# A retention layer with a feed-forward layer behind it: the order of three group sums on VectorE, and the place of one weight difference on GpSimd

## The chip, the cores and the metric

The kernel runs on one core of a Trainium2 chip. A core has a matrix engine (TensorE, PE in the profile), a vector engine (VectorE, DVE), a scalar engine (ScalarE, ACT), a general engine (GpSimd, POOL) and an engine that issues transfers (SyncE, SP). Each runs its own instructions in order; they wait for one another on semaphores. SBUF is the memory on the core that all of them read, PSUM the one into which TensorE accumulates. The metric is the time of one execution on the device, in microseconds (us), as the median of several runs.

## The reference

The inputs are q, k and v of 4 batches, 8 heads, 768 positions and 64 channels, and the weights of a feed-forward layer, 512 to 2048 to 512. What is computed:

```python
gamma = 1.0 - 2.0 ** (-5.0 - np.arange(H))
for t in range(S):
    state = gamma * state + outer(k[:, :, t], v[:, :, t])
    y[:, :, t] = scale * einsum('bhd,bhde->bhe', q[:, :, t], state)
x = y.transpose(0, 2, 1, 3).reshape(B * S, H * D)      # 3072 tokens x 512
h = x @ w_in
g = np.maximum(h, 0.0) + alpha * np.minimum(h, 0.0)
out = g @ w_out
```

The inputs and the output are float32; inside, the kernel multiplies in float16.

## The kernel before, in words

The 3072 tokens are cut into 24 units of 128 tokens and 6 blocks (n = 0 to 5) of 512 tokens. For each unit the retention part is done in chunks: scores within the chunk, masked, and a running state between chunks. Its result is written as xT, the input of the feed-forward layer for that block. The feed-forward layer of a block has two stages: `h = x @ w_in` with the activation, which leaves `gt` (2048 channels by 512 tokens, kept as 16 tiles f of 128 channels), and `g @ w_out`. The retention work of block n + 1 is woven into the second stage of block n.

The second stage of blocks 1 to 5 (`seven`, L802) is a product of 2 x 2 quarter matrices made with seven products in place of eight. `gt` is cut into four quarters: tokens 0 to 255 or 256 to 511 (`t0`, `t1`), and channel tiles 0 to 7 or 8 to 15 (`f`, `f8`). The seven products need four sums of these quarters, made by `g_sums(n, part, which, eng)` (L782): sum 0 is (`t1`, `f`) plus (`t1`, `f8`); sum 1 is sum 0 less (`t0`, `f`); sum 2, called `third`, is (`t0`, `f`) less (`t1`, `f`); sum 3 subtracts sum 1 from (`t0`, `f8`) in place. In the profile the tiles of sums 0 and 1 are called `gs`. `part` is 0 or 1 for half of the channel tiles, or None for all. `eng` is the engine, V for VectorE and G for GpSimd. `seven` asks first for two products that need no sum (32 matmuls), then for the product of sum 1 (16 matmuls: four of part 0, four of part 1, and the same again for the next 128 tokens), then for that of sum 0.

The first stage of blocks 3 to 5 (`ffn1_mix`, L918) treats a quarter of the channel tiles in the same way, and for that needs four differences and sums of w_in, which are made once (`win_sum(i, eng)`, L889, tile `wins`), and four differences of x for each block (`x_sum`, L902, tile `xsum`). The steps run in the order of the list `MIX`; its steps 5 and 6 read `wins` 0 and 1, step 7 reads `wins` 2, and step 3, the eleventh of the list, reads `wins` 3. GpSimd finishes three pairs of activations for these steps (two instructions each, L1002 and L1008).

All sums, of `gt`, of w_in and of x, go through one helper with one instruction, so all of them stand at L757 in the profile:

```python
def minus(eng, out, a, b, op=SUB):
    eng.tensor_tensor(out=out, in0=a, in1=b, op=op)
```

The order of the work on each engine is the order in which the program text issues it; no planner changes it. What a waiting instruction holds up is what is written behind it for the same engine. The places that matter here:

- In block 1, GpSimd makes sum 0 of part 0 (L1268) while the last activations of the block are still on VectorE. VectorE then makes sum 1 of part 0, sum 0 of part 1 and sum 1 of part 1 (L1313 to L1316). Blocks 2 to 4 make sums 0 and 1 whole on VectorE, with `part` None.
- In block 2, GpSimd makes the third sum of part 0 (L1291) and then the four differences of w_in (L1292).
- At the end of block 2's second stage, VectorE makes differences 0 and 1 of block 3's x, and GpSimd differences 2 and 3 (L1410 to L1413). What GpSimd does next is in block 3: the scaling of k and q of its last unit, behind which SP issues that unit's transpose and the loads of the next four units; then the three pairs of activations; then the third sum of part 0.

Of the kernel before, what the change touches and what calls it, by code (L numbers as in the profile page):

```python
# [19 lines left out]
def kernel(  # L20
# [72 lines left out]
    def bank(i, name, dt=FP, n=512):  # L93
        return psp.tile([128, n], dt, tag=f"p{i % 4}", bufs=1, name=name)
# [59 lines left out]
    def turn(u):  # L154
        kqT[u] = sbp.tile([128, 8, 128], F16, tag="kt", bufs=4, name=f"kt{u}")
        nc.sync.dma_start_transpose(
            out=kqT[u], in_=kqs[u].rearrange("p a i r d -> p (a i r d)")
        )
# [469 lines left out]
    def ffn1(n, lo=0, fts=None):  # L628
        for ft in fts or range(lo, NFT):
            hps = ps("hps", tag="pb")  # L630
            for hp in range(4):
                nc.tensor.matmul(  # L632
                    out=hps,
                    lhsT=w_in_all[:, hp, 128 * ft : 128 * ft + 128],
                    rhs=xT[n][:, :, hp, :],
                    start=(hp == 0),
                    stop=(hp == 3),
                )
                if hp == 3:
                    hm = sbp.tile([128, TB], FP, tag="hm", bufs=3, name="hm")  # L640
                    nc.scalar.activation(out=hm, in_=hps, func=RELU, bias=0.0, scale=-1.0)  # L641
                    nc.vector.scalar_tensor_tensor(  # L642
                        out=gt_at(n, ft, slice(0, TB)),
                        in0=hm,
                        scalar=oma_sb[:, ft : ft + 1],
                        in1=hps,
                        op0=MULT,
                        op1=ADD,
                    )
                yield  # L650
# [105 lines left out]
    def minus(eng, out, a, b, op=SUB):  # L756
        eng.tensor_tensor(out=out, in0=a, in1=b, op=op)  # L757
# [131 lines left out]
    def win_sum(i, eng):  # L889
        if not wins:  # L890
            wins.append(sbp.tile([128, 4, 2, 256], F16, tag="gs2", bufs=1, name="wins"))
        t = wins[0]
        a = [[w_in_all[:, 2 * l : 2 * l + 2, 1024 * j : 1024 * j + 256] for l in range(2)] for j in range(2)]
        x, y, op = (
            (a[1][0], a[1][1], ADD),
            (t[:, 0], a[0][0], SUB),
            (a[0][0], a[1][0], SUB),
            (a[0][1], t[:, 1], SUB),
        )[i]
        minus(eng, t[:, i], x, y, op=op)  # L900

    def x_sum(n, i, eng=nc.vector):  # L902
        if not xsum:
            xsum.append(sbp.tile([128, 4, 2, 256], F16, tag="gs3", bufs=1, name="xsum"))
        t = xsum[0]
        b = [[xT[n][:, j, 2 * l : 2 * l + 2, :] for j in range(2)] for l in range(2)]
        x, y = (
            (b[0][1], b[0][0]),
            (b[1][1], t[:, 0]),
            (b[1][1], b[0][1]),  # L910
            (b[1][0], t[:, 1]),
        )[i]
        minus(eng, t[:, i], x, y)
# [109 lines left out]
    def flush(late):  # L1023
        while late:
            late.pop(0)()

    def tick(gen, m):
        for _ in range(m):
            if next(gen, 1) == 1:
                return  # L1030
# [60 lines left out]
    V, G, A = nc.vector, nc.gpsimd, nc.scalar  # L1091
# [182 lines left out]
    for n in range(1, NBLK):  # L1274
        more = n + 1 < NBLK
        u0 = UB * (n + 1)
        if n == 2:
            gen = ffn1(n, fts=[HF * (f % 2) + f // 2 for f in range(NFT)])
            tick(gen, 8)
            flush(late_stores)  # L1280
            tick(gen, 6)
            for i in range(UB):
                scaled(u0 + i, "k", G)
                scaled(u0 + i, "q", G)
                turn(u0 + i)
                cast(u0 + i, G)

                for u in ((), (0,), (), (1, 2, 3))[i]:
                    load(u0 + u + UB)
                tick(gen, (14, 14, 6, 16)[i])  # L1290
            g_sums(n, 0, 2, G)  # L1291
            for i in range(4):  # L1292
                win_sum(i, G)
            for _ in gen:
                pass
        elif n > 2:
            gen = ffn1_mix(n)
            tick(gen, 8)
            flush(late_stores)
            if more:  # L1300

                scaled(u0 + 3, "k", G)
                scaled(u0 + 3, "q", G)
                turn(u0 + 3)
            for u in range(u0 + UB, min(u0 + 2 * UB, NU)):
                load(u)
            for _ in gen:
                pass
        if more:
            us = [u0, u0 + 1]  # L1310
            pq = scores(us)
            states(us)
        for p, w in (  # L1313
            ((0, 1), (1, 0), (1, 1)) if n == 1 else ((None, 0), (None, 1)) if more else ((1, 0), (1, 1))
        ):
            g_sums(n, p, w, V)  # L1316
        gen = seven(n)
        if not more:
            tick(gen, 4 * HF + 2)
            g_sums(n, 0, 2, V)  # L1320
            g_sums(n, 1, 2, V)
            g_sums(n, 0, 3, V)
            g_sums(n, 1, 3, V)
        if more:
            pa, pb = [u0, u0 + 1], [u0 + 2, u0 + 3]
            if n > 2:
                for u in pb:
                    cast(u, A)


            nxt = [u for u in range(u0 + UB, u0 + UB + 3) if n > 1 and u < NU]

            def chain(us, pq, first=(), between=(), last=(), ticks=0):
                sums(us[0])
                for g in first:
                    g_sums(n, *g)
                tick(gen, ticks)
                masked(us, pq)
                for g in between:
                    g_sums(n, *g)  # L1340
                for u in last:
                    scaled(u, "q", G)
                    turn(u)
                sums(us[1], late=n > 1 and us is pb)

            if n > 1:

                chain(pa, pq, [(1, 2, G)], ticks=4 * HF + 2)
                for u in nxt[0:1]:
                    scaled(u, "k", A)  # L1350
                tick(gen, 26)
                g_sums(n, 0, 3, G)
            else:
                tick(gen, 4 * HF // 2 + 1)
                scaled(11, "q", A)
                turn(11)
                for u in range(12, 16):
                    load(u)
                cast(10, A)
                cast(11, A)  # L1360
                tick(gen, 16)
                g_sums(n, 1, 3, G)
                chain(pa, pq, between=[(0, 2, V)])
                g_sums(n, 1, 2, V)
                tick(gen, 31)


            y = [bank(turns[0] + 2, "ya"), bank(turns[0] + 3, "yb")]
            out_first(pa, y)
            for X in range(2):  # L1370
                nc.scalar.activation(
                    out=seen[:, 8 * X : 8 * X + 8],
                    in_=y[X][:, 63:512:64],
                    func=COPY,
                    bias=0.0,
                    scale=1.0,
                )
            if n > 1:
                pq = scores(pb)
                states(pb)  # L1380
                out_second(pa)
            else:
                states(pb)
                out_second(pa)
                pq = scores(pb)
            if n > 1:
                chain(pb, pq, [], [(1, 3, G)], nxt[0:1])
            else:
                chain(pb, pq)
                g_sums(n, 0, 3, G)  # L1390
            tick(gen, 6)
            for u in nxt[0:2]:
                cast(u, A)
            for u in nxt[1:3]:
                scaled(u, "q", G)
            if n > 1:
                tick(gen, 15)
                decay(pb[1])
            for u in nxt[1:2]:
                scaled(u, "k", A)  # L1400
                turn(u)
            tick(gen, 17 if n > 1 else 23)
            out_first(pb, z=[ps("za"), ps("zb")])
            out_second(pb)
            for u in nxt[2:3]:
                scaled(u, "k", A)
                turn(u)
            tick(gen, 7)
            if n > 1:
                x_sum(n + 1, 0)  # L1410
                x_sum(n + 1, 1)
                x_sum(n + 1, 2, G)
                x_sum(n + 1, 3, G)  # L1413
        for _ in gen:
            pass
    flush(late_stores)
# [30 lines left out]
```

## Time and profile before

| what | us |
|---|---|
| median of 3 runs | 197.99 |
| the three runs | 197.58, 197.99, 487.58 |
| the profiled execution, its own time | 198.98 |
| span of the profiled execution, from its first to its last instruction | 197.0 |
| TensorE busy in that span | 189.3 |
| VectorE busy | 151.3 |
| GpSimd busy | 147.5 |
| ScalarE busy | 121.7 |

TensorE's granted clock is 1.000 over the whole span. The profiled execution's own time is 1.98 us longer than its span, which is what lies around the first and the last instruction. Rows of the timeline give the start in us from the span's begin, the length in us, the engine, the line, the operation, the tile written and the tiles read, the shape and the count; the bracket gives the idle time before the row and what ended it. Several instructions of one kind in a row are merged into one row, whose length runs from the start of the first to the end of the last.

### The profile page before, as it was taken

What the parts mean: (1) busy time and instruction counts of PE and PEld (TensorE: products, weight loads), DVE (VectorE), ACT (ScalarE), POOL (GpSimd) and SP (SyncE); (2) the same over time, 40 slices, a digit from 0 to 9 for tenths busy, and PEclk for the clock granted to TensorE, in tenths of its full rate; (3) what the DMA queues carried; (4) which work ended last, traced back from release to release, by engine and by line L of the source; (5) the groups of instructions that cost most, each with busy time, mean ns of one, the idle gap of its engine ahead of it and who ended that gap; (6) DMA issues with size and microseconds to landing.
All of it is one profiled execution on the core that took longest, in us unless ns stands there. A gap on an engine that the chain in (4) does not pass through costs nothing.

```text
span 197.0 us, 6461 instructions
## 1 busy us (share of the span) xinstructions
PE 189.3 (96%) x2668; PEld 131.7 (67%) x2668; DVE 151.3 (77%) x260; ACT 121.7 (62%) x272; POOL 147.5 (75%) x148
## 2 busy tenths in 40 slices
PE   7789899999999989999999999999999999999993
PEld 5657444557768878744688754788754888654882
DVE  2597889253999698588897879968879977799943
ACT  3368664349687863476458988749987433687120
POOL 3286788999996955999659999579999397589000
PEclk9999999999999999999999999999999999999999
DMA  6999999999999989899999999993890011200014
GB/s 168 310 336 350 404 396 296 332 358 179 210 230 148 214 257 272 196 215 299 196 231 228 226 185 265 237 221 93 113 263 2 3 57 63 100 3 0 2 57 160
DMA packets 92749, 38.78 MB, mean 197 GB/s; under 512 B 70176, under 2 KB 88624, under 8 KB 92720
## 3 DMA queue, kind: packets, MB, share of 16 engines
q1 hardware_dynamic: 91440, 37.36, 77.2%
q10 hardware_dynamic: 1280, 1.01, 1.5%
q8 instruction: 21, 0.34, 0.7%
q14 instruction: 8, 0.07, 0.1%
HBM read 27.35 MB, written 6.29 MB: 171 GB/s over the span
## 4 chain that ended last, share of the span: by engine, by line
PE 73%; SPq 10%; DMA 7%; POOL 6%; DVE 1%; issue 1%; POOLq 0%
PE ops L809 30%; PE hps L942 16%; PE hps L632 12%; PE hps L972 5%; SPq L340 4%; SPq L117 4%; DMA wi<-in_moe_w_in_dram 4%; PE ops L734 4%; POOL wsum L757 3%; DMA kqs<-in_q_dram 3%; PE ya L293 1%; PE yb L293 1%; POOL gs L757 1%; DVE gs L757 1%; POOL ukq L354 1%; PE sca L234 1%
## 5 line engine op out<-in xcount | busy, mean ns | idle before, releaser
L809 PEld LDWEIGHTS <-gt 128*128 128x128 f16 x320 | 30.6, 98 | 4.2
L942 PE MATMUL hps<-xT,win 128*128 128x512 f16 x144 | 33.0, 379 | 0.0
L929 DVE SCALAR_TENSOR_TENSOR gt<-hm,small,hps 128x512 f16<-128x512 f32 (+1 forms) x42 | 28.7, 706 | 5.1 <-ACT hm L925 3.8
L809 PE MATMUL ops<-wout,gt 128*128 128x256 f16 x240 | 28.4, 273 | 0.0
L925 ACT ACTIVATE hm<-hps 128x512 f32<-128x512 f32 x39 | 23.1, 593 | 6.1 <-PE hps L942 5.4
L632 PE MATMUL hps<-xT,win 128*128 128x512 f16 x112 | 24.7, 379 | 0.6 <-POOL win L1073 0.6
L137 POOL TENSOR_TENSOR kq<-kqs,tab 128x512 f16<-128x512 f32 x23 | 23.7, 1051 | 1.9 <-DMA kqs<-in_q_dram 1.9
L642 DVE SCALAR_TENSOR_TENSOR gt<-hm,small,hps 128x512 f16<-128x512 f32 x28 | 20.9, 748 | 3.8 <-ACT hm L641 0.9
L942 PEld LDWEIGHTS <-win 128*128 128x128 f16 x144 | 14.1, 98 | 14.5
L641 ACT ACTIVATE hm<-hps 128x512 f32<-128x512 f32 x28 | 16.7, 597 | 8.9 <-PE hps L632 8.6
L674 DVE SCALAR_TENSOR_TENSOR gt<-hm,small,hps 128x256 f16<-128x256 f32 x40 | 16.9, 476 | 5.0 <-ACT hm L669 5.0
L827 ACT ACTIVATE kept<-ops 128x512 f32<-128x512 f32 x15 | 9.0, 597 | 18.8 <-PE ops L809 18.7
L632 PEld LDWEIGHTS <-win 128*128 128x128 f16 x112 | 10.9, 98 | 13.6 <-POOL win L1073 1.1
L809 PE MATMUL ops<-wsum,gs 128*128 128x256 f16 x160 | 19.0, 273 | 0.7 <-DVE gs L757 0.7
L217 POOL TENSOR_TENSOR t<-ss,tab 128x256 f16<-128x256 f32 x13 | 8.7, 669 | 13.6 <-DVE ss L215 13.6
L757 POOL TENSOR_TENSOR gt<-gt,gs 128x1024 f16<-128x1024 f16 x8 | 17.0, 2126 | 2.2 <-DVE gs L757 2.2
L660 PE MATMUL hps<-xT,win 128*128 128x256 f16 x160 | 18.4, 273 | 0.0
L129 ACT ACTIVATE kq<-kqs,tab 128x64 f16<-128x64 f32 x72 | 18.0, 336 | 0.0
L660 PEld LDWEIGHTS <-win 128*128 128x128 f16 x160 | 15.4, 98 | 2.6 <-DVE xT L584 0.3
L809 PEld LDWEIGHTS <-gs 128*128 128x128 f16 x160 | 15.1, 98 | 3.0 <-DVE gs L757 1.0
L669 ACT ACTIVATE hm<-hps 128x512 f32<-128x512 f32 x20 | 11.8, 597 | 4.5 <-PE hps L660 4.4
L839 DVE TENSOR_TENSOR os<-ops,kept 128x512 f32<-128x512 f32 (+1 forms) x17 | 10.5, 624 | 5.0 <-ACT kept L827 3.7
(139 smaller groups left out, 391.5 us busy)
## 6 DMA issues: line engine op xcount, KB each, us to landing
out_dram<-os SPq DMA_DIRECT2D x20, 256.0 KB, 3.6
wi<-in_moe_w_in_dram SPq DMA_DIRECT2D x8, 512.0 KB, 8.6
wo<-in_moe_w_out_dram SPq DMA_DIRECT2D x8, 512.0 KB, 8.7
kqs<-in_k_dram SPq DMA_DIRECT2D x16, 256.0 KB, 4.4
kqs<-in_q_dram SPq DMA_DIRECT2D x16, 256.0 KB, 4.3
vs<-in_v_dram SPq DMA_DIRECT2D x16, 256.0 KB, 4.7
ku<-in_k_dram SPq DMA_DIRECT2D x4, 256.0 KB, 4.4
qu<-in_q_dram SPq DMA_DIRECT2D x4, 256.0 KB, 5.3
```

The costliest lines, as they stand in the source:

```text
L129: eng.activation(out=kqs[u][:, a, h % 4, h // 4, :], in_=staged[u][nm][:, h, :], func=COPY, bias=0.0, scale=tab[:, H * a + h : H * a + h + 1],
L137: eng.tensor_tensor(out=kqs[u][:, a].rearrange("p i r d -> p r i d"), in0=staged[u][nm].rearrange("p (r i) d -> p r i d", i=4), in1=tab[:, ...
L632: nc.tensor.matmul(out=hps, lhsT=w_in_all[:, hp, 128 * ft : 128 * ft + 128], rhs=xT[n][:, :, hp, :], start=(hp == 0), stop=(hp == 3),)
L641: nc.scalar.activation(out=hm, in_=hps, func=RELU, bias=0.0, scale=-1.0)
L642: nc.vector.scalar_tensor_tensor(out=gt_at(n, ft, slice(0, TB)), in0=hm, scalar=oma_sb[:, ft : ft + 1], in1=hps, op0=MULT, op1=ADD,)
L660: nc.tensor.matmul(out=hps[:, 256 * (ft - f0) : 256 * (ft - f0) + 256], lhsT=w_in_all[:, hp, 128 * ft : 128 * ft + 128], rhs=xT[n][:, half ...
L674: nc.vector.scalar_tensor_tensor(out=gt_at(n, f, to), in0=hm[:, at], scalar=oma_sb[:, f : f + 1], in1=hps[:, at], op0=MULT, op1=ADD,)
L757: eng.tensor_tensor(out=out, in0=a, in1=b, op=op)
L809: nc.tensor.matmul(out=bk[:, 256 * t : 256 * t + 256], lhsT=a[:, f, 128 * t : 128 * t + 128], rhs=w[:, f, :], start=first and f == 0 and ( ...
L925: nc.scalar.activation(out=t, in_=src, func=RELU, bias=0.0, scale=-1.0)
L929: nc.vector.scalar_tensor_tensor(out=gt_at(n, f, cols), in0=hm, scalar=oma_sb[:, f : f + 1], in1=src, op0=MULT, op1=ADD,)
L942: nc.tensor.matmul(out=hps, lhsT=w_in_all[:, hp, 128 * ft : 128 * ft + 128], rhs=x[:, :, hp, :], start=(hp == 0), stop=(hp == 3),)
```

## The change: what it does

Two things are changed. In block 1, VectorE's three group sums get another order: sum 0 of part 1 comes first, then sum 1 of part 0, then sum 1 of part 1. Of these only sum 1 of part 0 reads what GpSimd writes. And GpSimd makes difference 3 of w_in not in block 2 behind the other three, but at the end of block 2's second stage, behind the differences of block 3's x. No instruction is added, removed or given to another engine.

```diff
@@ block 2, first stage
             g_sums(n, 0, 2, G)
-            for i in range(4):
+            for i in range(3):
                 win_sum(i, G)
@@ before the second stage
         for p, w in (
-            ((0, 1), (1, 0), (1, 1)) if n == 1 else ((None, 0), (None, 1)) if more else ((1, 0), (1, 1))
+            ((1, 0), (0, 1), (1, 1)) if n == 1 else ((None, 0), (None, 1)) if more else ((1, 0), (1, 1))
         ):
             g_sums(n, p, w, V)
@@ end of the second stage
                 x_sum(n + 1, 2, G)
                 x_sum(n + 1, 3, G)
+                if n == 2:
+                    win_sum(3, G)
```

## The prediction

> **What bounds the kernel now.** I read the page first, its busy times and then its chain of work that ended last.
>
> ```profile
> span 197.0 us, 6461 instructions
> ...
> PE 189.3 (96%) x2668; PEld 131.7 (67%) x2668; DVE 151.3 (77%) x260; ACT 121.7 (62%) x272; POOL 147.5 (75%) x148
> ...
> PE 73%; SPq 10%; DMA 7%; POOL 6%; DVE 1%; issue 1%; POOLq 0%
> ```
>
> TensorE is busy for 96% of the span and carries 73% of the chain. So a microsecond counts only where TensorE waits for it, and the other engines count where they hold TensorE up. Next I read the chain in order of time around block 1, with the timelines of TensorE, VectorE and GpSimd at that place (start, length, then what ran).
>
> ```profile
> 68.77 1.30 DVE gs L757 x2
> ...
> 70.84 3.23 PE ops L809 x28
> ```
>
> ```profile
> 59.43 7.64 DVE L674 SCALAR_TENSOR_TENSOR gt<-hm,small,hps 128x256 f16<-128x256 f32 x18 [0.31 <-ACT hm L669]
> 68.77 0.69 DVE L757 TENSOR_TENSOR gs<-gs,gt 128x1024 f16<-128x1024 f16 x1 [1.69 <-POOL gs L757]
> 69.38 0.68 DVE L757 TENSOR_TENSOR gs<-gt 128x1024 f16<-128x1024 f16 x1
> 70.09 0.69 DVE L757 TENSOR_TENSOR gs<-gs,gt 128x1024 f16<-128x1024 f16 x1
> ...
> 73.28 0.89 DVE L757 TENSOR_TENSOR third<-gt 128x1024 f16<-128x1024 f16 x1
> ```
>
> ```profile
> 69.56 0.60 PE L809 MATMUL ops<-wsum,gs 128*128 128x256 f16 x4
> 70.84 3.23 PE L809 MATMUL ops<-wsum,gs 128*128 128x256 f16 x28 [0.68 <-DVE gs L757]
> ```
>
> ```profile
> 66.61 2.12 POOL L757 TENSOR_TENSOR gs<-gt 128x1024 f16<-128x1024 f16 x1
> ...
> 73.01 0.61 POOL L217 TENSOR_TENSOR t<-ss,tab 128x256 f16<-128x256 f32 x1
> ```
>
> The reader is to see three things. VectorE ends its activations at 67.07 (59.43 + 7.64) and idles 1.69 us for GpSimd's half of sum 0, which ends at 68.73. It then makes sum 1 of part 0, sum 0 of part 1 and sum 1 of part 1. TensorE starts on part 0 without a wait and idles 0.68 us for part 1, whose sum is ready at 70.78. This is the stall that the new order aims at, and the rest of the block hangs on it.
>
> **Block 1: the new order.** Nothing is added or removed; three VectorE instructions change places. If VectorE had its data path to itself, sum 0 of part 1 would run from 67.10 to 67.78 inside the idle time, and the last sum would follow part 0's directly: it would start at 69.38 in place of 70.09. That is 0.71 us, the upper bound of the gain.
>
> But GpSimd is then in the middle of its own sum, and the trace shows what happens when VectorE reads two operands from SBUF beside it.
>
> ```profile
> 167.58 0.42 DVE L757 TENSOR_TENSOR xsum<-xT 128x512 f16<-128x512 f16 x1
> 168.11 1.28 DVE L757 TENSOR_TENSOR xsum<-xT,xsum 128x512 f16<-128x512 f16 x1
> ```
>
> ```profile
> 167.95 1.15 POOL L757 TENSOR_TENSOR xsum<-xT 128x512 f16<-128x512 f16 x1 [1.90 <-ACT xT L612]
> ```
>
> ```profile
> 33.18 1.89 DVE L757 TENSOR_TENSOR wsum<-wout 128x2048 f16<-128x2048 f16 x1
> ```
>
> ```profile
> 32.95 1.04 POOL L354 TENSOR_TENSOR ukq<-ku,tab 128x512 f16<-128x512 f32 x1 [0.40 <-DMA ku<-in_k_dram]
> 33.95 2.02 POOL L354 TENSOR_TENSOR ukq<-ku,tab 128x512 f16<-128x512 f32 x1
> ```
>
> The VectorE sum of 512 elements takes 0.42 us alone, and 1.28 us when it starts during a GpSimd instruction that ends at 169.10. It ends 0.29 us after GpSimd does. The sum of 2048 elements behaves the same way: GpSimd's first instruction ends at 33.99, and VectorE ends 1.08 us later, at 35.07. GpSimd's next instruction, started at 33.95, takes 2.02 us in place of 1.04: it waits for VectorE in its turn. For 1024 elements the row at 73.28 gives the remainder: GpSimd ends at 73.62, VectorE at 74.17, so 0.55 us. I read this as a lock: whoever came second runs when the first is through.
>
> So sum 0 of part 1 starts at 67.10, is held until 68.73 and ends at 69.28. Sum 1 of part 0 follows at 69.21 (independent neighbours start 0.08 us before the other ends: 69.38 against 69.46) and ends at 69.90, later than now by 0.44. The last sum starts at 69.82 and ends at 70.51, earlier by 0.27. TensorE begins part 0 at about 69.96, needs 0.60 for its four matmuls and goes on at 70.57 in place of 70.84. **I take a gain of 0.27 us.** The lower bound is a loss of 0.06: the held sum takes 0.68 after 68.73, and each of the next two starts 0.02 behind the other's end, so the last ends at 70.84. I take the value near the lower end because three overlaps in this trace ended within the remainders above. What follows on VectorE, ACT and GpSimd in this block is released by these sums and by TensorE, so it moves with them.
>
> **Weighed against a page.** The Trainium skill, SBUF — State Buffer, section "Who interferes with whom", says that a VectorE instruction with two SBUF inputs contends with a GpSimd instruction that reads SBUF, and that the second to issue blocks fully until the first is through. The trace agrees on the blocking; if the whole instruction came after it (0.68 and 1.23 us where the rows have 0.55 and 1.08), the sum below would be 199.07 in place of 198.80.
>
> **Blocks 2 and 3: the moved w_in difference.** These are the rows of GpSimd, then of VectorE, TensorE, SP's queue and ScalarE.
>
> ```profile
> 95.52 1.16 POOL L757 TENSOR_TENSOR wins<-win,wins 128x512 f16<-128x512 f16 x1
> 100.58 0.61 POOL L217 TENSOR_TENSOR t<-ss,tab 128x256 f16<-128x256 f32 x1 [3.90 <-DVE ss L215]
> ...
> 112.48 1.15 POOL L757 TENSOR_TENSOR xsum<-xT 128x512 f16<-128x512 f16 x1
> 113.60 1.16 POOL L757 TENSOR_TENSOR xsum<-xT,xsum 128x512 f16<-128x512 f16 x1
> 114.71 2.05 POOL L137 TENSOR_TENSOR kq<-kqs,tab 128x512 f16<-128x512 f32 x2
> ...
> 117.83 1.27 POOL L1008 TENSOR_TENSOR gt<-hm,kept 128x512 f16<-128x512 f32 x1
> ...
> 123.89 2.13 POOL L757 TENSOR_TENSOR third<-gt 128x1024 f16<-128x1024 f16 x1
> 129.34 0.61 POOL L217 TENSOR_TENSOR t<-ss,tab 128x256 f16<-128x256 f32 x1 [3.33 <-DVE ss L215]
> ```
>
> ```profile
> 97.15 1.22 DVE L757 TENSOR_TENSOR gs<-gt 128x2048 f16<-128x2048 f16 x1
> ...
> 125.92 1.23 DVE L757 TENSOR_TENSOR gs<-gt 128x2048 f16<-128x2048 f16 x1
> 127.18 1.23 DVE L757 TENSOR_TENSOR gs<-gs,gt 128x2048 f16<-128x2048 f16 x1
> ```
>
> ```profile
> 112.42 1.18 PE L972 MATMUL hps<-xsum,wins 128*128 128x256 f16 x8
> ...
> 116.89 0.60 PE L972 MATMUL hps<-xT,wins 128*128 128x256 f16 x4
> ```
>
> ```profile
> 128.48 3.22 PE L809 MATMUL ops<-wsum,gs 128*128 128x256 f16 x28
> ```
>
> ```profile
> 117.47 1.30 SPq L156 DMA_TRANSPOSE kt<-kq  x1
> ```
>
> ```profile
> 119.86 0.63 ACT L925 ACTIVATE hm<-kept 128x512 f32<-128x512 f32 x1
> ```
>
> Where it leaves, nothing is gained: the difference ends at 96.68, before VectorE's sums start at 97.15, and GpSimd then idles 3.90 us for VectorE anyway.
>
> Where it arrives, GpSimd has no idle time from 100.58 to the end of its third sum at 126.02. The difference starts at 114.71 and pushes everything behind it by 1.12 (the spacing of 112.48 and 113.60). What stands behind: two scalings of unit 19, on which SP's transpose and four units' loads wait; three pairs that finish activations; and the third sum. All but the last are covered. TensorE reads the new difference at 116.89, and it ends at 115.87. SP's transpose is ready at 117.88 in place of 116.76 but stands in its queue until 117.47, so it and the loads behind it slip 0.4 us, and unit 19 is wanted only with block 3's second score products, past 130. ScalarE's third relu reuses the buffer of the first pair, free at 120.22 in place of 119.10, so it starts 0.36 us late; that stays below the wait that comes next.
>
> The third sum is not covered. It would run from 125.01 to 127.14, and VectorE asks for its sum 0 of 2048 elements at 125.92, in the middle. By the lock it is held until 127.14 and ends 1.08 us later, at 128.22, against 127.15 now: 1.07 us late. Sum 1 depends on it and ends at 129.48 in place of 128.41. TensorE took it at 128.48, so there is no slack. **I take a loss of 1.07 us.** The lower bound is 0 (VectorE not held), the upper 1.22 (held, then 1.23 in full). A gain is excluded, since TensorE did not wait there. Later, GpSimd idles 3.33 us to 129.34 for VectorE, so the delay of GpSimd itself ends there, and all engines go on behind the same sum: I see nothing that gives the 1.07 back.
>
> **Sum.** The profiled execution took 198.98 us, a span of 197.0 and 1.98 around it. With −0.27 and +1.07 it becomes 199.78, a span of 197.8. The median of the runs, 197.99, lies 0.99 below this execution; I predict on the median: 197.99 + 0.80 = 198.79, rounded to 198.8.
>
> **The rivals.** First, that VectorE is not held at either place, because these two sums get by GpSimd's: block 1 gives its full 0.71, block 3 costs nothing, 197.99 − 0.71 = 197.3. Against it stand the three overlaps above; for it, that none of them pairs sums as long as GpSimd's 2.12 us with VectorE's. Chance 0.14.
>
> Second, that the change does not collide in block 3. If GpSimd's third sum slips another 0.91 us, past 125.92, VectorE comes first and GpSimd waits, at no cost, since it is idle until 129.34. Only block 1's gain is left, 197.7. Against it: nothing between 115.87 and 125.01 waits longer than those 0.36 us. Chance 0.12.
>
> Third, on the slow side: that TensorE's products at 112.42 wait for the whole tile of w_in differences, now complete at 115.87, and not for their own quarter. That costs 3.45 us and moves VectorE's sums clear of GpSimd's third: 197.99 − 0.27 + 3.45 = 201.2. It is decided by whether the difference ends after 112.42, which it does. Against it: the same products read their quarter of the x sums at 112.42 while GpSimd writes another quarter of that tile at 112.48. Chance 0.04.
>
> **How the numbers follow.** My forecast has 0.66, a remainder of 0.04 is unnamed. Its own range: from the gain's upper bound with the loss as taken, 198.35, to both bad bounds, 199.27; with the 0.41 us between the two undisturbed runs (197.58 and 197.99) that is 197.9 to 199.7. With the first two rivals the range is 197.2 to 199.8, which leaves out the third, the remainder and some tails. About 2% is what a measurement of this kernel can tell from no change; that is 194.0 and 202.0. No case reaches the first. The third rival comes within 0.8 of the second. Faster 0.01, within 2% 0.96, slower 0.03.
>
> **What would show it.** In block 1, VectorE's sum 0 of part 1 starts near 67.1 and takes some 2.2 us; a length of 0.68 means the first rival. TensorE's part 0 starts near 70.0 and its wait for part 1 is gone. In block 3, GpSimd's third sum starts near 124.7 (0.27 earlier, with block 1's gain) and VectorE's sum 0 grows from 1.23 to some 2.3 us, with an idle TensorE for about 1.1 us before the next products. If that sum keeps its 1.23 us, the loss is wrong; if TensorE idles near 112, the third rival is right.

## The result, and the profile after

The changed kernel took 200.79 us (median of 6 runs), the kernel before 198.52 in the runs of that comparison (197.99 in the three shown earlier). The ratio is 1.0105, with a 95% interval of 1.0057 to 1.0152: slower by some 2 us, where 0.8 us and 198.8 had been predicted and a range up to 199.8. It was compared twice more, beside the experiments: 1.0083 (1.0051 to 1.0116) and 1.0051 (1.0016 to 1.0085). So the direction holds each time, and the size lies between 1.0 and 2.1 us. Ratios, intervals and spreads leave out slow executions, those over 1.5% above the fastest of their kernel; of the profiles, only that of the kernel with all four sums on VectorE is of such an execution.

The page of the changed kernel, profiled in an execution of 201.2 us:

```profile
span 199.2 us, 6461 instructions
...
PE 188.4 (95%) x2668; PEld 131.1 (66%) x2668; DVE 151.8 (76%) x260; ACT 121.6 (61%) x272; POOL 147.8 (74%) x148
```

The span is 2.2 us longer, and no engine is busier by more than 0.5 us. Block 1, in the timelines of VectorE, GpSimd and TensorE:

```profile
69.20 0.97 DVE L757 TENSOR_TENSOR gs<-gt 128x1024 f16<-128x1024 f16 x1
70.10 1.28 DVE L757 TENSOR_TENSOR gs<-gs,gt 128x1024 f16<-128x1024 f16 x2
```

```profile
67.50 2.13 POOL L757 TENSOR_TENSOR gs<-gt 128x1024 f16<-128x1024 f16 x1 [0.41 <-DVE gt L674]
```

```profile
68.15 3.67 PE L809 MATMUL ops<-wout,gt 128*128 128x256 f16 x32
71.66 3.66 PE L809 MATMUL ops<-wsum,gs 128*128 128x256 f16 x32
```

VectorE's first sum starts before GpSimd's has ended (69.63) and ends 0.54 us after it, at 70.17, as the prediction's lock has it. TensorE goes from the first row to the second without an idle time, and the 32 matmuls of sums 1 and 0 run as one group: the wait of 0.68 us is gone. But the first row starts at 68.15, where the corresponding row of before starts at 66.06:

```profile
66.06 3.67 PE L809 MATMUL ops<-wout,gt 128*128 128x256 f16 x32
```

So this execution was 2.09 us late before the first changed instruction. The waits of TensorE say where most of it arose:

```profile
PE sca L483 <- DMA ukT<-ukq: 1.8, 1, 1.8
```

That is a wait for the transposes of an earlier unit. It ends at 53.85, in block 1's first stage, where both kernels run the same instructions. The first profile of before has no such wait. Then block 3:

```profile
126.08 2.13 POOL L757 TENSOR_TENSOR third<-gt 128x1024 f16<-128x1024 f16 x1
```

```profile
127.87 1.42 DVE L757 TENSOR_TENSOR gs<-gt 128x2048 f16<-128x2048 f16 x1
```

VectorE's sum is held until GpSimd ends at 128.21, and ends 1.08 us later, but it is only 0.19 us longer than before, not 1.07. VectorE asked later than predicted, because the kernel had waited in block 2, for something the prediction had not looked at. ScalarE's copies of v in block 2, for units 16 and 17, before in one row:

```profile
105.29 1.15 ACT L150 ACTIVATE vx<-vs 128x512 f16<-128x512 f32 x2
```

and in the changed kernel, with the load it waited for in the chain of work (start and length of the transfer):

```profile
108.01 0.63 ACT L150 ACTIVATE vx<-vs 128x512 f16<-128x512 f32 x1 [1.01 <-DMA vs<-in_v_dram]
```

```profile
102.66 5.27 DMA vs<-in_v_dram
```

### The profile page after: what moved, and what is told of

Same layout as the page of the kernel before. It is cut to its first block, busy times and chain, and to the rows that moved or that the text cites. A ratio compares the mean times of both kernels' runs of the same rounds, so it can differ in the third digit from the quotient of the medians.

```text
span 199.2 us, 6461 instructions
## 1 busy us (share of the span) xinstructions
PE 188.4 (95%) x2668; PEld 131.1 (66%) x2668; DVE 151.8 (76%) x260; ACT 121.6 (61%) x272; POOL 147.8 (74%) x148
## 4 chain that ended last, share of the span: by engine, by line
PE 57%; DMA 14%; SPq 13%; POOL 6%; ACT 6%; issue 2%; DVE 0%; ACTq 0%
PE ops L809 19%; PE hps L942 15%; SPq L117 6%; PE hps L632 5%; DMA wi<-in_moe_w_in_dram 5%; PE hps L660 4%; SPq L340 4%; DMA ukT<-ukq 4%; PE hps L972 4%; PE ops L734 4%; ACT kq L129 4%; DMA vs<-in_v_dram 3%; DMA kqs<-in_k_dram 2%; SPq L156 2%; PE ops L696 2%
## 5 line engine op out<-in xcount | busy, mean ns | idle before, releaser
L942 PEld LDWEIGHTS <-win 128*128 128x128 f16 x144 | 14.1, 98 | 14.4
```

Of the source, the lines that this page charges most:

```text
L942: nc.tensor.matmul(out=hps, lhsT=w_in_all[:, hp, 128 * ft : 128 * ft + 128], rhs=x[:, :, hp, :], start=(hp == 0), stop=(hp == 3),)
```

## The experiments

Two theories stood at the start. A: the change costs what its two parts do to each other's engines, and the rest of the 2 us is chance ahead of it. B: the change itself costs 1%.

**The kernel before and the changed kernel again, and each part alone.** The edits of the two parts:

```diff
-            ((0, 1), (1, 0), (1, 1)) if n == 1 ...      # order only
+            ((1, 0), (0, 1), (1, 1)) if n == 1 ...
```

```diff
-            for i in range(4):              # move only
+            for i in range(3):
                 win_sum(i, G)
...
                 x_sum(n + 1, 3, G)
+                if n == 2:
+                    win_sum(3, G)
```

> The kernel before, unchanged, as a control. Theory A (what came in the changed profile ahead of block 1 is chance): its executions spread over some 3 us, and a profiled one can lie 2 us late at block 1's first second-stage matmul (66.06 in the first profile of before, 68.15 in that of the changed kernel), with TensorE waiting at line 483 for the transposes of unit 3. Theory B (the change costs 1% by itself): the spread of this kernel is small, its ratio is 1.000 within 0.3%, and that point lies at 66.1 +- 0.3 again.

> The changed kernel once more. Theory A: ratio near 1.000 to 1.004; from block 1's first second-stage matmul to the end it takes 130.1 to 131.9 us, against 130.94 before. Theory B: ratio 1.010 again, and the stretch behind that point is some 2 us longer than before.

> Only the new order of VectorE's sums in block 1; w_in's difference stays in block 2. Theory A: block 1 gains 0.27 us if GpSimd's sum starts ahead of VectorE's first one by 0.5 us as in the first profile, up to 1 us if it starts later; ratio 0.995 to 0.999. VectorE's first sum lasts until 0.55 us after the end of GpSimd's. Theory B with the order to blame: ratio 1.010.

> Only the place of w_in's difference. By the prediction's step: in block 3 VectorE's sum 0 of 2048 elements lasts until 1.08 us after the end of GpSimd's third sum, up to 2.3 us long, TensorE idles up to 1.07 us in front of sum 1's product, ratio 1.001 to 1.005. If the delay of GpSimd is taken up on its way, that sum keeps 1.23 us and the ratio is 1.000. Theory B with the move to blame: ratio 1.010.

Measured: before again 1.0015 (0.998 to 1.0049), the changed kernel 1.0083 (1.0051 to 1.0116), the order alone 1.0021 (0.998 to 1.0061), the move alone 1.0056 (1.0026 to 1.0086). The 22 runs of the kernel before that count beside them reach from 196.46 to 199.28 us, a spread like the one that theory A names. The control's profile comes to block 1 at 65.42, neither 2 us late nor at 66.1. Neither theory comes out whole. The changed kernel lies above A's 1.004 and below B's 1.010, while its stretch from block 1 on takes 131.03 us, within what A expected. Theory B does not hold for the order, whose interval ends below 1%; but the gain expected from the order does not show in its runs either, only in its profile, where block 1 is short (table below). The move alone costs 0.56% where the whole change costs 0.83%; the two intervals overlap, so the move's share is not settled by the runs.

In the move alone, GpSimd's third sum and VectorE's sum 0 of block 3, with TensorE's only wait from block 1 on:

```profile
123.12 2.12 POOL L757 TENSOR_TENSOR third<-gt 128x1024 f16<-128x1024 f16 x1
```

```profile
124.19 2.13 DVE L757 TENSOR_TENSOR gs<-gt 128x2048 f16<-128x2048 f16 x1
```

```profile
PE ops L809 <- DVE gs L757: 0.7, 1, 0.7
```

GpSimd ends at 125.24, VectorE at 126.32, 1.08 us later, and TensorE idles for it: the prediction's step, nearly whole. The changed kernel's second profile has the same pair with a length of 1.90 us in place of 2.13.

```profile
124.57 2.13 POOL L757 TENSOR_TENSOR third<-gt 128x1024 f16<-128x1024 f16 x1
```

```profile
125.88 1.90 DVE L757 TENSOR_TENSOR gs<-gt 128x2048 f16<-128x2048 f16 x1
```

The order alone shows the lock of block 1 by itself. GpSimd's sum ends at 67.22 and VectorE's at 67.77, 0.55 us later.

```profile
65.10 2.12 POOL L757 TENSOR_TENSOR gs<-gt 128x1024 f16<-128x1024 f16 x1
```

```profile
66.54 1.23 DVE L757 TENSOR_TENSOR gs<-gt 128x1024 f16<-128x1024 f16 x1
```

**VectorE makes all four sums of block 1; a short and a long delay of GpSimd's third sum; the changed kernel once more.** The first drops `g_sums(1, 0, 0, G)` and gives VectorE the list `((0, 0), (0, 1), (1, 0), (1, 1))`. The delays are fills in block 3 (one or four), all else as before:

```diff
 +            if s == 15 and n == 3:
+                pad = sbp.tile([128, 1024], F16, tag="pad", name="pad")
+                for _ in range(1):          # range(4) for the long delay
+                    nc.gpsimd.memset(pad, 1.0)
             if s == 15:
                 g_sums(n, 0, 2 if n + 1 < NBLK else 0, nc.gpsimd)
```

> From the kernel before: in block 1 VectorE makes sum 0 of part 0 too (four sums of 0.69 us instead of three), GpSimd none, and w_in's difference stays in block 2. If what held the sums in block 1 is GpSimd's 2.12 us instruction (as a wait in the old order, as a lock in the new one), no sum is held: each takes 0.68 to 0.69 us from the end of the last activation, part 1 is ready 2.8 us after it, TensorE does not wait at line 809, and the stretch from block 1's first second-stage matmul to block 2's first matmul is 14.65 us, as in the order-only run, against 15.67 and 15.03 in the two profiles of before. Ratio 0.995 to 0.999. If the fourth sum costs more than the lock, TensorE idles in front of part 0 and the stretch is over 15.0.

> From the kernel before: one GpSimd fill of 1024 elements of a tile that nobody reads, in block 3 just ahead of the third sum (about 1.1 us; w_in's difference stays in block 2). If the move costs by the delay of that third sum alone, this costs the same as the move: VectorE's sum 0 lasts until 1.08 us after the third sum's end, 1.9 to 2.3 us, the products of sum 1 come 4.2 to 4.5 us after the two products before them (3.51 before), ratio 1.002 to 1.005. If the move costs by the difference itself being late or by what stands behind it, this kernel keeps 3.51 and ratio 1.000.

> The same with four fills (about 4.4 us). If the lock goes to whoever asks first, the longer delay costs less than the short one: VectorE asks first, its two sums keep 1.23 us each beside the fills, which read nothing, GpSimd's third sum waits or comes after them, the products of sum 1 come 3.5 us after the two products before them, and at most 0.3 us is lost later in block 3 since GpSimd's decay of the state comes 1 us late. Ratio 0.999 to 1.003. If a late GpSimd costs by its lateness, this kernel loses about 4 times the short one, ratio over 1.006.

> The changed kernel a third time, for where its time lies. By the stages of the profiles so far, from block 1's first second-stage matmul to the end it takes 131.0 us (before 130.5 to 130.9), and what its totals have above that came ahead of that point, where both kernels run the same instructions: then that point lies at 66.0 to 68.2 again by chance, and the ratio may fall to 1.002 to 1.006. If the totals are right and the change costs 1.6 us, the stretch behind that point is 131.5 us or more here.

Measured: all four sums on VectorE 1.0001 (0.9968 to 1.0035), the short delay 1.0049 (1.0008 to 1.0089), the long one 1.003 (0.9988 to 1.0071), the changed kernel 1.0051 (1.0016 to 1.0085).

With all four on VectorE none is held, as expected, and block 1 takes 14.66 us. The ratio misses its expectation of 0.995 to 0.999, so here too the short block 1 does not show in the runs:

```profile
68.75 0.68 DVE L757 TENSOR_TENSOR gs<-gt 128x1024 f16<-128x1024 f16 x1
69.47 0.69 DVE L757 TENSOR_TENSOR gs<-gs,gt 128x1024 f16<-128x1024 f16 x1
70.08 0.68 DVE L757 TENSOR_TENSOR gs<-gt 128x1024 f16<-128x1024 f16 x1
70.80 0.69 DVE L757 TENSOR_TENSOR gs<-gs,gt 128x1024 f16<-128x1024 f16 x1
```

The long delay shows who wins the lock. First the rows of GpSimd, then those of VectorE:

```profile
121.57 3.99 POOL L1019 MEMSET pad<- 128x1024 f16 x4
125.52 2.73 POOL L757 TENSOR_TENSOR third<-gt 128x1024 f16<-128x1024 f16 x1
```

```profile
123.78 1.23 DVE L757 TENSOR_TENSOR gs<-gt 128x2048 f16<-128x2048 f16 x1
125.04 1.22 DVE L757 TENSOR_TENSOR gs<-gs,gt 128x2048 f16<-128x2048 f16 x1
```

Fills, which read nothing, leave VectorE's sums at 1.23 and 1.22 us. GpSimd's third sum, which now comes second, takes 2.73 us in place of 2.13: it waits until VectorE ends at 126.26. The products of sum 1 come without a wait. So the third sum costs at this place when it is there first and still running, not because it is late. The long delay does lose 0.75 us further on (last column of the table below, 69.27 against 68.52), where at most 0.3 us was expected.

The short delay missed its expectation: VectorE's sum kept 1.23 us. In that execution ScalarE waited 0.93 us for v of unit 17 in block 2, TensorE and VectorE came late, and VectorE asked 0.09 us before GpSimd was done. So this profile tells nothing of the delay, but it shows that a wait for v can take the place of the wait at the lock. The changed kernel's third profile is such a case too (a wait for v of 1.25 us, no time on the lock).

**A program with one idle instruction more; v of unit 17 loaded first.** The wait for v stands in all three profiles of the changed kernel and in neither of the unedited kernel before. The load stands behind k and q of its unit on SP's queue. One experiment keeps the work and only adds an idle instruction; the others change the order of the three transfers (the body of `load` follows the string that it is given):

```diff
-                    load(u0 + u + UB)
+                    load(u0 + u + UB, "vkq" if u == 1 else "kqv")
```

> The kernel before with one GpSimd fill of 16 elements added behind all its work, which nothing waits for: the same work otherwise. Every edited kernel so far came out 0.3 to 0.8 us above what its stages from block 1 on explain. Theory C (any other program than before's own runs its first 66 us a little slower): ratio 1.002 to 1.005. Theory D (those excesses are chance or lie behind block 1): ratio 1.000 within 0.003.

> Only the new order in block 1, and in block 2 SP loads v of unit 17 ahead of its k and q (before: behind them), since in the changed kernel ScalarE waited 0.5 to 1.25 us for that load. If block 1's gain is given back in block 2 to that load: the stretch from block 2's second stage to block 3's first matmul is 14.3 to 14.4 us in every profile (15.09, 14.60 and 15.32 in the changed kernel), the gain stays, ratio 0.994 to 0.998. If something else takes it, the ratio stays at 1.002 as for the order alone.

> The changed kernel with v of unit 17 loaded first. If the late w_in difference makes GpSimd's row of work from 101 to 128 us the bound, taking away the wait for v gives nothing: block 2's stretch shortens to 14.3 to 14.4 us, block 3's products of sum 1 come 4.1 to 4.4 us after the two before them (3.5 to 4.2 in the changed kernel), and from block 2's second stage to those products it takes 33.2 to 33.3 us as before; ratio 1.003 to 1.007. If the wait for v was what the change cost, those products come at 3.5 and the ratio is at most 1.002.

> VectorE makes all four sums of block 1, v of unit 17 is loaded first, w_in's difference stays in block 2: a version meant to beat both kernels. No stretch from block 1 on waits for GpSimd or for v: 14.65, 14.55, 14.3 to 14.4, 14.29 and 3.5 us, from block 1's first second-stage matmul to the end 129.8 us; ratio 0.993 to 0.998. If the edits cost in the first 66 us what they save behind, ratio 1.000.

Measured: the idle instruction 1.0009 (0.9976 to 1.0042), as theory D has it; the interval does not shut out the lower part of theory C. The order with v first 0.9992 (0.9958 to 1.0026), the changed kernel with v first 1.0034 (1.0001 to 1.0067), all four sums on VectorE with v first 0.9986 (0.9949 to 1.0023). Both versions that were expected to beat the kernel before missed: neither is clear of it, and their stretch of block 2 took 14.56 and 14.76 us, not 14.3 to 14.4, though neither waited for v.

In the changed kernel with v first (its line numbers are one higher) the wait for v is gone. The lock comes back at nearly full price, and the ratio stays where the first of the two cases expected it:

```profile
125.22 2.13 POOL L758 TENSOR_TENSOR third<-gt 128x1024 f16<-128x1024 f16 x1
```

```profile
126.16 2.27 DVE L758 TENSOR_TENSOR gs<-gt 128x2048 f16<-128x2048 f16 x1
```

```profile
PE ops L810 <- DVE gs L758: 0.9, 1, 0.9
```

**All profiles by stages.** Each number is a difference of two starts of TensorE's rows, as 15.67 for before: 81.73, where block 2's first stage starts, less 66.06. "Block 1" runs from the first matmul of its second stage to the first of block 2; block 2's first stage, which takes 14.54 to 14.55 us everywhere, is left out. "Block 2" runs from its second stage to block 3's first matmul, "block 3" from there to its second stage, "to sum 1" from there to the products of sum 1. The sum is that of these three columns, the rest goes to the end of the span.

| kernel | block 1 starts at | block 1 | block 2 | block 3 | to sum 1 | sum | rest |
|---|---|---|---|---|---|---|---|
| before | 66.06 | 15.67 | 14.40 | 14.29 | 3.51 | 32.20 | 68.52 |
| before again | 65.42 | 15.03 | 14.56 | 14.29 | 3.51 | 32.36 | 68.54 |
| idle instruction | 65.43 | 14.65 | 15.04 | 14.48 | 3.50 | 33.02 | 68.55 |
| short delay | 66.97 | 14.76 | 15.01 | 14.47 | 3.50 | 32.98 | 68.54 |
| long delay | 64.90 | 14.65 | 14.44 | 14.29 | 3.50 | 32.23 | 69.27 |
| order | 65.49 | 14.65 | 14.32 | 14.29 | 3.53 | 32.14 | 68.47 |
| order, v first | 65.50 | 14.65 | 14.56 | 14.30 | 3.51 | 32.37 | 68.53 |
| all four on VectorE | 67.81 | 14.66 | 14.49 | 14.29 | 3.50 | 32.28 | 68.51 |
| all four on VectorE, v first | 65.67 | 14.65 | 14.76 | 14.29 | 3.50 | 32.55 | 68.48 |
| move | 65.19 | 14.66 | 14.56 | 14.28 | 4.40 | 33.24 | 68.46 |
| changed | 68.15 | 14.65 | 15.09 | 14.48 | 3.69 | 33.26 | 68.59 |
| changed again | 66.57 | 14.74 | 14.60 | 14.47 | 4.17 | 33.24 | 68.50 |
| changed, third | 67.11 | 14.65 | 15.32 | 14.48 | 3.50 | 33.30 | 68.49 |
| changed, v first | 67.30 | 14.65 | 14.43 | 14.29 | 4.53 | 33.25 | 68.55 |

The column "sum" is the finding. With the moved difference it is 33.24 to 33.30 in all five profiles. In four of them GpSimd sets it: its third sum ends 30.84 us after block 2's second stage starts in the move alone (125.24 less 94.40) and 30.86 us in the changed kernel (128.21 less 97.35), against 29.74 before (126.02 less 96.28), and VectorE's held sum ends 1.08 us behind it. In the changed kernel's third profile GpSimd ends as late (30.85), but VectorE asked 0.11 us before that end and its sum kept 1.23 us; there the wait for v alone took about as long. Without the move the sum lies between 32.1 and 33.0, the upper values where v was late.

## Why the prediction was right or wrong

**The lock.** Right in both places and in its sizes: sums that were held ended 0.54 to 0.55 us (1024 elements) and 1.08 us (2048) after GpSimd; only where VectorE asked some 0.1 us before GpSimd's end did its sum keep its 1.23 us. The first rival falls with that. The second falls because GpSimd's third sum was there before VectorE's in every profile with the move. Its mechanism exists, as the long delay shows; but there GpSimd, delayed by 4 us and not by 2, lost 0.75 us further on, so that the rival's "at no cost" is not shown. What the Trainium skill's page named in the prediction (SBUF — State Buffer, section "Who interferes with whom") says is borne out by runs that the prediction did not have: the second to ask waits, on either engine, and GpSimd's fills, which only write, do not hold VectorE (1.23 and 1.22 us beside them). The price of the wait is that of the rows, not of a whole instruction.

**The loss of 1.07 us in block 3.** The mechanism is right, and with nothing else in the way the price nearly too: 0.9 us in the move alone (4.40 against 3.51), 1.02 in the changed kernel with v first. As a step of a sum it was too simple. The delay of GpSimd makes a floor of some 33.25 us under that stretch; what it costs is 33.25 less what the stretch takes without the move, by the profiles here 0.2 to 1.1 us. The third rival is wrong: in the profiles with the move TensorE has no wait near block 3's first products beyond 0.2 us.

**The gain of 0.27 us in block 1.** Near on the average, and by luck. The old order's six profiles (both of before, idle instruction, both delays, move) take 14.90 us there on the average, the new order's six (order, order with v first, and the changed kernel in its four profiles) 14.67. But the stall that the order removes is in two of the old order's six only: against 14.65 they take 1.02 and 0.38 us more, the others at most 0.11. And the totals do not show the gain, with 1.0021 and 0.9992 for the two kernels with the order alone. In the first profile, on which the sum was worked out, GpSimd was late for a load:

```profile
61.44 1.04 POOL L137 TENSOR_TENSOR kq<-kqs,tab 128x512 f16<-128x512 f32 x1 [1.54 <-DMA kqs<-in_q_dram]
```

In the move alone, by contrast, its sum waited for VectorE's activations, not for a transfer:

```profile
64.48 2.13 POOL L757 TENSOR_TENSOR gs<-gt 128x1024 f16<-128x1024 f16 x1 [0.49 <-DVE gt L674]
```

**"So it moves with them."** The sentence is about VectorE, ACT and GpSimd and leaves out SP. SP's queue of block 2 does not follow block 1's sums. Its first transpose starts 4.48 to 4.49 us after block 1's second stage does, in all profiles, and from there transfer follows transfer. The load of v for unit 17 is issued 33.92 us after that start in before (99.98 less 66.06) and 34.51 in the changed kernel (102.66 less 68.15):

```profile
99.98 1.11 SPq L117 DMA_DIRECT2D vs<-in_v_dram  x1
```

With block 1 a microsecond shorter, ScalarE also wants it earlier. So part of the gain can come back as a wait in block 2. It does not always: with the three transfers in their old order the load is issued anywhere from 32.5 to 34.6 us after that start, and ScalarE waited in the five profiles where it was 34.0 or later. All three of the changed kernel are among them, but so are the idle instruction and the short delay, with the old order of the sums and no stall to speak of.

**The sum, and where it failed.** The two terms make +0.80 us. In the first pair of profiles the stages show −1.02 us in block 1 and +1.06 in the stretch up to sum 1's products, and 0.11 us in all from block 1 on. So the terms do not explain the 2.1 us of the first comparison, and that the third comparison's 1.0 us is near 0.80 is luck. The step that failed is one that the prediction put at nothing: that the changed kernel comes to block 1 when the kernel before does. Its only allowance was a scatter of 0.41 us, taken from two runs. Of the 2.2 us between the first two profiles, 2.09 lie ahead of that start. Before's own runs spread over 2.8 us (196.46 to 199.28), and block 1 starts anywhere from 64.90 to 68.15 us in profiles that run the same instructions up to there.

What stays open: from block 1 on, the changed kernel's three profiles take 131.0 us each, before's two 130.94 and 130.48 and the idle instruction's 130.77, so about 0.3 us of the 1.0 to 2.1 show there. The rest shows ahead of it, where the four profiles with both parts start block 1 at 66.57 to 68.15 and the two of before at 66.06 and 65.42. Three of these four have the wait at line 483 seen above (1.8, 1.3 and 1.6 us; 484 with v first); of the other ten profiles only one has it (1.0 us, all four sums on VectorE with v first). An idle instruction behind all other work does not bring this about (1.0009). Whether it is chance, or something that the change does to the start of the program, was not settled.

## What to carry to other kernels

Before an order is changed to fill one engine's idle time, look at what the other reader of the same memory is doing then: an instruction placed there may only wait in another place. On an engine with no idle time an inserted instruction puts a floor under the whole stretch, and what it costs depends on how far the other waits of the stretch reach already. A stall in one profile may hang on a load that was late in that execution; a second profile of the same kernel is the cheapest guard, and the spread of its runs belongs in the range.

## What the runs showed of the hardware

A GpSimd fill of 1024 float16 elements takes about 1.0 us (3.99 us for four) and did not hold VectorE's sums of two SBUF operands, while a GpSimd sum of as many elements (2.13 us) holds them to its end. Of a held VectorE sum 0.55 us remain after that end, of 0.68 alone, and 1.08 of 1.23; that its start is hidden in the wait is a reading of these numbers.
